# Matrix balancing on 32 partitions against 128 partitions in two halves, at the head of a fused attention and gated-MLP kernel

## The chip, the core and the metric

The kernel runs on one core of a Trainium2 chip. A core has a matrix engine (TensorE, "PE" in the profile, with its weight loads as "PEld"), a vector engine (VectorE, DVE), an activation engine (ScalarE, ACT), a general engine (GpSimd, POOL) and a synchronisation engine (SyncE, SP), each with an instruction queue of its own that it works through in order, and 16 DMA engines that all queues share. Matrix products land in PSUM, which PE alone writes by products and which ACT and DVE read; everything else lives in SBUF. The metric is the device time of one execution in microseconds (us). The kernel before takes 232.88 us, the median of three runs (232.8 to 232.88).

## What is computed

The reference balances a small 8x8 matrix for each of 4 batches x 8 heads by five rounds of exponential, row normalisation and column normalisation. The result mixes the eight blocks (96 positions each) of the keys and of the values; block-diagonal attention follows, and then a two-layer gated MLP.

```python
P = sort_net                                   # (4, 8, 8, 8)
for _ in range(5):
    P = P - np.max(P, axis=-1, keepdims=True)
    P = np.exp(P)
    P = P / (np.sum(P, axis=-1, keepdims=True) + 1e-09)
    P = P / (np.sum(P, axis=-2, keepdims=True) + 1e-09)
...
k_sorted = np.einsum('bhij,bhjcd->bhicd', P, k_b)
v_sorted = np.einsum('bhij,bhjcd->bhicd', P, v_b)
scores = scale * np.matmul(q_b, k_sb.transpose(0, 1, 2, 4, 3))
attn = exp(scores - rowmax) / (rowsum + 1e-09)
x = attn @ v_sb                                # 3072 tokens x 512
h = x @ w_in                                   # 512 x 2048
out = (h * np.cos(h)) @ w_out                  # 2048 x 512
```

## The kernel before

The 3072 tokens go in eight chunks `n` of 384, two for each batch; a chunk has four blocks `u` of 96 positions. The order of the instructions on every engine is the order in which the program text issues them. The text from line 77 to line 990 or so is the head of the kernel: inputs are loaded, the matrices are balanced, the keys and values of batch 0 are mixed, and attention of chunk 0 is computed. With `up_four(0, 0, 0)` (line 982) begins the MLP of chunk 0, and from there on pieces of attention for later chunks are placed between the MLP's products.

**Balancing.** `P` (line 80) holds one (batch, head) pair on each of 32 partitions, 64 numbers in a row. `rounds(it)` (line 334) runs five times: an exponential on ACT, then `normalize` (line 307), six DVE instructions: sum, reciprocal, product for the rows, and the same for the columns. The last product writes `sorted_by` in bf16. To bring the 8x8 matrices of 16 (batch, head) pairs into the block-diagonal form that a product over 128 partitions needs, `block` (line 380) makes eight products of 8 columns with the 0/1 matrices `pick`, built on POOL (`picked`, line 211), and `spread` (line 391) multiplies the result with the mask `maskp` into `bds[0]` (keys), `bdv` (values) and, much later (line 1024), `bds[1]` (batches 2 and 3). Between these steps the rounds carry other work: `q_twice` and `q_place` (transposes of q for chunk 0 on PE, copies on ACT), the clearing of halves of `kbuf` and `vbuf` on POOL, loads of `w_in`, and `idle(...)`, products without use on PE.

**Loads.** All large loads are issued on POOL's queue and converted to bf16 on the way: `load_q(0)`, K and V of batch 0 (lines 190 to 192), then three quarters of `w_in`, held back by a copy (`held`, line 368) that waits for a column reciprocal of the second round, the fourth quarter behind the fourth round, `load_q(1)` (line 378), four pieces of `v_permute`, `w_out` (lines 925 to 930), and K and V of batch 1 (lines 968 and 970). `P` itself comes on SP's queue.

**Keys, values, scores.** `kp` (line 744) multiplies 16 columns of keys with `bds[0]` into a PSUM tile; `k_place` copies it to `kT` on ACT or DVE, in two parts `half` for the first and last four blocks. `s_ps`, `s_max` and `s_sub` make the scores of a block, their row maxima, and the differences; `expo` makes the exponential. `expo(..., True)` leaves the transposing of the probabilities to PE (`p_ps`) and a copy (`p_ev`); without `True` it issues a DMA transpose on SP's queue. `v0` and `v0e` mix the values of batch 0; `av_products`, `av_norm` (line 614 on), `x_ps` and `x_ev` make the attention output and its transpose for the MLP. `q_products(1, 0, ...)` at line 977 transposes the second load of q on PE.

**PSUM.** Two pools: `big` with three tiles of two banks, `acc` with two tiles of one bank. A tile is given out again when its last reader in program order has passed.

Of the kernel before, what the change touches and what calls it, by code (L numbers as in the profile page):

```python
# [18 lines left out]
def kernel(  # L19
# [15 lines left out]
    nc = tc.nc  # L35
# [155 lines left out]
    load(kbuf, 64, kin_d[0])  # L191
    load(vbuf, 0, vin_d[0])
    make_identity(nc, ident[:])
# [5 lines left out]
    zero_words(nc.gpsimd, kbuf[:64, :CD // 3])  # L199
# [4 lines left out]

    def pick_at(z, n):
        return pair[:B * H, z * PB * nb:(z + n) * PB * nb].rearrange(
            "p (j c) -> p j c", j=nb)

    pick, pick_pair = pick_at(0, 2), pick_at(2, 2)

    def picked(t, z, b):

        nc.gpsimd.affine_select(
            out=t[:, :, z * PB:(z + 1) * PB], in_=t[:, :, z * PB:(z + 1) * PB],
            compare_op=ALU.not_equal, fill=1.0, base=-b * PB,
            pattern=[[1, nb], [-1, PB]], channel_multiplier=nb)

    def picks(t, batches):
        nc.gpsimd.memset(t[:], 0.0)
        for z, b in enumerate(batches):  # L220
            picked(t, z, b)
# [10 lines left out]
    nc.vector.memset(pick[:], 0.0)  # L232
# [7 lines left out]

    early = const.tile([128, 1], FP32, name="early")
    nc.scalar.activation(early[:], half_pi[:], AF.Exp)

# [6 lines left out]
    keep_warm(14, big.tile([128, 512], FP32, name="idle", tag="big"))  # L250
# [32 lines left out]
    E_eps = const.tile([B * H, nb, nb + 1], FP32, name="E")  # L283
    Q_eps = const.tile([B * H, nb + 1, nb], FP32, name="Q")
    E, Q = E_eps[:, :, :nb], Q_eps[:, :nb]
    top = const.tile([B * H, nb], FP32, name="top")
    less = const.tile([B * H, nb, nb], FP32, name="less")
    sums = [const.tile([B * H, nb], FP32, name=f"sums{z}") for z in range(2)]
    over = [const.tile([B * H, nb], FP32, name=f"over{z}") for z in range(4)]
    sorted_by = const.tile([B * H, nb, nb], BF16, name="sorted_by")  # L290
    maskp = const.tile([128, 2 * H], FP32, name="maskp")
    bds = [const.tile([128, 2 * H, nb], BF16, name=f"bd{g}") for g in range(NG)]
    bdv = const.tile([128, 2 * H, nb], BF16, name="bdv")
    held = const.tile([128, 1], FP32, name="held")

    def by_row(t):
        return t.to_broadcast([B * H, nb, nb])

    def by_column(t):
        return t[:].unsqueeze(1).to_broadcast([B * H, nb, nb])  # L300

    nc.vector.memset(E_eps[:, :, nb:], 1e-9)
    nc.vector.memset(Q_eps[:, nb:], 1e-9)
    nc.vector.reduce_max(top[:], P[:], axis=AX.X)
    nc.vector.tensor_tensor(less[:], P[:], by_row(top), op=ALU.subtract)

    def normalize(it, out):

        nc.vector.reduce_sum(sums[0][:], E_eps[:], axis=AX.X)
        nc.vector.reciprocal(over[0][:], sums[0][:])  # L310
        nc.vector.tensor_tensor(Q, E, by_row(over[0]), op=ALU.mult)
        nc.vector.reduce_sum(sums[1][:], Q_eps.rearrange("p i j -> p j i"), axis=AX.X)
        nc.vector.reciprocal(over[(1, 2, 1, 3, 1)[it]][:], sums[1][:])
        nc.vector.tensor_tensor(out, Q, by_column(over[(1, 2, 1, 3, 1)[it]]), op=ALU.mult)

    turns = {}

    def q_twice(h2):
        ps = turns[h2] = acc.tile([128, 2, IC, QR, blk // QR], BF16, name="qps", tag="acc")
        for hp in range(2):  # L320
            for r in range(QR):
                for x in range(2):
                    nc.tensor.transpose(
                        ps[x * D:(x + 1) * D, hp, :, r],
                        q_rows[:, h2 * 2 + hp, r * D:(r + 1) * D], ident[:blk, :blk])

    def q_place(h2):
        dst = q_turned[0][:, :, :QW].rearrange("d e (i h c) -> d h e i c", h=H2, c=blk)
        A.copy(dst[:, h2], turns.pop(h2).rearrange("d e i r p -> d e i (r p)"))
# [4 lines left out]
    def rounds(it):  # L334
        nc.scalar.activation(E, less[:], AF.Exp)
        if it == 0:
            A.copy(
                order.rearrange("k (p r) -> k p r", r=QR),
                ident[:blk, :blk].rearrange("k (r p) -> k p r", r=QR))
            q_twice(0)  # L340
            q_twice(1)
            idle(4)
        if it == 3:
            q_place(0)
            q_twice(2)
            idle(2)
            q_place(1)
            q_twice(3)
            idle(2)
        if it == 4:  # L350
            q_place(2)
            q_place(3)
        if it in (1, 2):
            n = (D - 12 - VN) // 2 * blk
            t = vperm[64:, VN * blk + (it - 1) * n:VN * blk + it * n].bitcast(FP32)
            A.copy(t, nones[64:].to_broadcast([64, n // 2]))
# [894 lines left out]
```

## Time and profile before

| what | before |
|---|---|
| median of three runs | 232.88 us |
| span of the profiled execution, first to last instruction | 231.6 us |
| PE busy | 223.5 us (97%) |
| DVE busy | 170.9 us (74%) |
| ACT busy | 154.2 us (67%) |
| POOL busy | 95.9 us (41%) |
| bytes moved by DMA | 31.21 MB |

The span is that of one profiled execution; its time outside the span isn't given by itself, so the difference to the median, 1.3 us, stands for what lies around it. A row of the timeline has the start and the duration in us, the engine, the line of the program, the operation, output and inputs, shapes and a count; in brackets stands how long the engine was idle before and what released it. Idle time of an engine that isn't the bound costs nothing.

### The profile page before, as it was taken

How to read it: one execution, taken by the hardware profiler on the slowest of the kernel's cores; microseconds unless marked ns; L12 is line 12 of the kernel's file. 1: busy time of each engine (PE TensorE's matmuls, PEld its weight loads, DVE VectorE, ACT ScalarE, POOL GpSimd, SP SyncE). 2: the span in 40 equal slices, each digit the busy share in tenths (PEclk: the TensorE clock that was granted, in tenths of full speed). 3: DMA queues.
4: the chain of work that ended last, by engine and by line, in shares of the span. 5: the costliest groups of instructions: out<-in, count | busy, mean ns of one | idle time of the engine just before them, and what ended most of it. 6: DMA issues, size and time to landing. Idle time of an engine off the chain costs nothing.

```text
span 231.6 us, 5534 instructions
## 1 busy us (share of the span) xinstructions
PE 223.5 (97%) x2268; PEld 138.9 (60%) x2268; DVE 170.9 (74%) x291; ACT 154.2 (67%) x207; POOL 95.9 (41%) x121
## 2 busy tenths in 40 slices
PE   8888999999999999999999999999999999999994
PEld 3477898567665566644666456555655566556553
DVE  6769968978789778877389986997699769745700
ACT  5658877777789858794888566746675666716521
POOL 7999999399950188932709000900000000000000
PEclk9999999999999999999999999999999999999999
DMA  5999999994999999797989839964923450351012
GB/s 69 230 191 207 202 207 233 199 225 139 125 135 172 174 137 148 130 168 158 154 138 89 122 72 146 215 90 92 207 91 69 90 167 0 68 146 45 0 45 93
DMA packets 67673, 31.21 MB, mean 135 GB/s; under 512 B 56384, under 2 KB 63168, under 8 KB 67392
## 3 DMA queue, kind: packets, MB, share of 16 engines
q0 software_dynamic: 24048, 13.64, 43.5%
q1 hardware_dynamic: 43312, 17.02, 35.1%
q8 instruction: 18, 0.29, 0.5%
q10 hardware_dynamic: 288, 0.20, 0.3%
q14 instruction: 7, 0.06, 0.1%
HBM read 27.27 MB, written 6.29 MB: 145 GB/s over the span
## 4 chain that ended last, share of the span: by engine, by line
PE 85%; DMA 5%; DVE 3%; POOL 2%; ACT 2%; issue 1%; SPq 1%; POOLq 0%; ACTq 0%
PE h L669 30%; PE o L694 28%; PE h L857 5%; PE o L878 5%; DMA kTs<-kTs 4%; PE av L625 3%; PE sc L438 3%; PE ks L408 2%; PE o L1215 2%; PE pps L835 1%; PE xps L656 1%; PE sc L504 1%; PE vs L782 1%; PE xps L844 1%; SPq L421 1%
## 5 line engine op out<-in xcount | busy, mean ns | idle before, releaser
L669 PE MATMUL h<-xT,w_in_t 128*128 128x384 bf16 x448 | 78.4, 326 | 0.0
L694 PE MATMUL o<-w_out_t,gg 128*128 128x512 bf16 x320 | 76.2, 379 | 0.0
L677 DVE TENSOR_TENSOR gg<-c,h 128x768 bf16<-128x768 f32 x56 | 52.7, 949 | 20.0 <-ACT c L673 20.0
L673 ACT ACTIVATE c<-h,half_pi 128x768 f32<-128x768 f32 x56 | 50.4, 900 | 25.3 <-PE h L669 24.4
L669 PEld LDWEIGHTS <-w_in_t 128*128 128x128 bf16 x448 | 42.2, 98 | 26.5 <-DMA xT<-xn 0.4
L694 PEld LDWEIGHTS <-gg 128*128 128x128 bf16 x320 | 28.9, 98 | 28.4
L179 POOL COPY vperm<-kv 64x768 bf16<-64x768 bf16 (+2 forms) x12 | 28.4, 2413 | 3.9 <-DMA kv<-in_v_dram 3.9
L570 ACT ACTIVATE p_buf<-s 96x768 bf16<-96x768 f32 x32 | 26.6, 842 | 5.1 <-DVE s L491 4.0
L489 DVE TENSOR_REDUCE mx<-sc 96x4 f32<-96x384 f32 (+1 forms) x33 | 24.0, 728 | 2.2 <-PE sc L504 2.2
L491 DVE TENSOR_TENSOR s<-sc,mx 96x384 f32<-96x384 f32 (+1 forms) x33 | 24.3, 735 | 1.6
L638 DVE TENSOR_TENSOR xn<-av,r 96x512 bf16<-96x512 f32 x32 | 22.0, 686 | 1.1
L129 POOL DMA_DIRECT2D kv<-in_q_dram x24 | 16.0, 680 | 0.8 <-issue 0.5
L257 ACT COPY kv<-o 128x512 f32<-128x512 f32 (+2 forms) x10 | 5.2, 523 | 14.1 <-PE o L694 11.5
L257 ACT CAST kTs<-ks 128x512 bf16<-128x512 f32 (+1 forms) x18 | 11.0, 630 | 5.3 <-PE ks L408 4.4
L636 DVE RECIPROCAL r<-av 96x8 f32<-96x8 f32 x32 | 6.4, 199 | 7.9 <-PE av L625 7.6
L878 PE MATMUL o<-w_out_t,gg 128*128 128x512 bf16 x48 | 11.7, 379 | 0.0
L438 PE MATMUL sc<-kTs,q_turned 128*128 128x96 bf16 x152 | 11.0, 206 | 0.5 <-DMA kTs<-kTs 0.5
L129 POOL DMA_DIRECT2D q_mem<-in_q_dram x16 | 10.7, 690 | 1.8 <-DMA kv<-in_v_dram 1.5
L259 DVE COPY kv<-o 128x512 f32<-128x512 f32 (+1 forms) x5 | 3.1, 612 | 11.1 <-PE o L1215 8.5
L857 PE MATMUL h<-xT,w_in_t 128*128 128x192 bf16 x128 | 11.1, 246 | 0.0
L438 PEld LDWEIGHTS <-q_turned 128*128 128x128 bf16 x152 | 8.8, 98 | 3.0 <-issue 0.6
L857 PEld LDWEIGHTS <-w_in_t 128*128 128x128 bf16 x128 | 10.5, 98 | 0.0
(134 smaller groups left out, 279.1 us busy)
## 6 DMA issues: line engine op xcount, KB each, us to landing
out_dram<-kv SPq DMA_DIRECT2D x12, 256.0 KB, 2.6
out_dram<-o_s SPq DMA_DIRECT2D x10, 256.0 KB, 3.1
w_in_t<-in_moe_w_in_dram POOLq DMA_DIRECT2D x4, 512.0 KB, 11.8
w_out_t<-in_moe_w_out_dram POOLq DMA_DIRECT2D x4, 512.0 KB, 12.4
kv<-in_k_dram POOLq DMA_DIRECT2D x2, 768.0 KB, 9.9
kv<-in_v_dram POOLq DMA_DIRECT2D x2, 768.0 KB, 13.0
pair<-in_k_dram POOLq DMA_DIRECT2D x2, 768.0 KB, 12.4
kv<-in_v_dram POOLq DMA_DIRECT2D x6, 256.0 KB, 5.7
```

Source lines behind the costliest of these rows:

```text
L129: nc.gpsimd.dma_start(out=q_heads[:, i, :, e], in_=src[:, ih * IC + i, :, e])
L179: nc.gpsimd.tensor_copy(dst, src)
L438: nc.tensor.matmul(out, q_of(n, hp)[:, x:x + 128], keys_of(n, u, h2, hp), start=True, stop=True)
L489: nc.vector.reduce_max(mx[:], scv, axis=AX.X)
L491: nc.vector.tensor_tensor(s, scv, mx.to_broadcast(list(s.shape)), op=ALU.subtract)
L570: nc.scalar.activation(p[:, :, :blk], s_t.pop((n, u)).rearrange("p e h c -> p (e h) c"), AF.Exp, scale=scale)
L669: nc.tensor.matmul(h[:, f2, :w], w_in_t[:, kk, f * 128:(f + 1) * 128], xT[n][:, kk], start=(kk == 0), stop=(kk == KC - 1))
L673: nc.scalar.activation(c[:], h[:, :, :w], AF.Sin, bias=half_pi[:, 0:1])
L677: nc.vector.tensor_tensor(gt[n, fp // 2][:, f:f + 2], c[:], h[:, :, :w], op=ALU.mult)
L694: nc.tensor.matmul(o[:], gt[n, f // 4][:, f % 4, ts * 128:(ts + 1) * 128], w_out_t[:, f, :], start=(f == 0), stop=(f == FC - 1))
L857: nc.tensor.matmul(o[:, part, f2 * w:(f2 + 1) * w], w_in_t[:, kk, f * 128:(f + 1) * 128], xT[0][:, kk, h * w:(h + 1) * w], start=(kk == 0) ...
L878: nc.tensor.matmul(out_ps[ts][:], gt[0, q][:, f % 4, ts * 128:(ts + 1) * 128], w_out_t[:, f, :], start=(f == 0), stop=(f == FC - 1))
```

## The change

`P` is loaded with one (batch of a pair, head, row) on each of 128 partitions, and the two pairs of batches (`g` = 0, 1) beside each other with 8 numbers each. The first exponential takes the row maximum as bias. The row sums of the first round are then sums along a partition; a product with a 128x128 fp32 matrix (`wide`) turns the matrices, so that from there on rows are columns: the column sums are sums along a partition, and their reciprocal becomes the scale of the next exponential, while the row sums are fp32 products with a 0/1 block matrix (`own`). The small constant of the reference enters through a product with ones (`start_rows`) ahead of each. The two halves take turns. The last reciprocal is multiplied in with the mask, so that `bds[0]` and `bds[1]` come directly out of the last round; `block`, `pick`, `bdv` and the later `picks` go. One matrix `bds[0]` serves keys and values.

Keys of batch 0 now lie on the first 64 partitions of `kbuf` and those of batch 1 on the others. Key copies use four PSUM tiles (16, 16, 8 and 8 columns) instead of three of 16. The probabilities of blocks 0 and 3 of chunk 0 are transposed by DMA instead of PE. The first warm-up has 9 products instead of 14, and the later `idle` and `fill` products of the head go. Some clearings move from POOL to DVE (`ident`, `p_bufs`, the ones in `vS`) or from ACT to DVE (half of a stretch of `vperm`), and ahead of the K and V loads POOL gets four small additions (`tree`).

```diff
-    P = const.tile([B * H, nb, nb], FP32, name="P")
-    nc.sync.dma_start(out=P.rearrange("p i j -> p (i j)"),
-                      in_=sort_net.rearrange("b h i j -> (b h) (i j)"))
+    P = const.tile([128, NG, nb], FP32, name="P")
+    nc.sync.dma_start(
+        out=P[:], in_=sort_net.rearrange("(g b) h i j -> (b h i) g j", g=NG))
...
     load_q(0)
-    load(kbuf, 64, kin_d[0])
+    nc.vector.memset(ident[:], 0.0)
+    nc.gpsimd.affine_select(
+        out=ident[:], in_=ident[:], compare_op=ALU.not_equal, fill=1.0, base=0,
+        pattern=[[-1, 128]], channel_multiplier=1)
+    tree = [const.tile([128, w + w // 8], FP32, name=f"tree{w}") for w in (64, 32, 16, 8)]
+    nc.vector.memset(tree[3][:, nb:], 0.0)
+    t = ident
+    for x, w in zip(tree, (64, 32, 16, 8)):
+        nc.gpsimd.tensor_tensor(x[:, :w], t[:, :w], t[:, w:2 * w], op=ALU.add)
+        t = x
+    place9 = tree[3]
+    load(kbuf, 0, kin_d[0])
     load(vbuf, 0, vin_d[0])
-    make_identity(nc, ident[:])
...
-    nc.vector.memset(pick[:], 0.0)
...
+    for t in p_bufs:
+        nc.vector.memset(t[:, :, blk:], 0.0)
...
-    keep_warm(14, big.tile([128, 512], FP32, name="idle", tag="big"))
+    keep_warm(9, big.tile([128, 512], FP32, name="idle", tag="big"))
...
+    def start_rows(g, lo, n):
+        nc.tensor.matmul(
+            turned[g][:, lo:lo + n], every, least[:, lo:lo + n], start=True, stop=False)
...
+    def turn_first(g):
+        nc.vector.reduce_sum(sums[:, g, 0:1], first[:, g], axis=AX.X)
+        nc.vector.reciprocal(over[:, g, 0:1], sums[:, g, 0:1])
+        shape = [128, 2 * H, nb]
+        nc.vector.scalar_tensor_tensor(
+            wide[g].rearrange("p (c j) -> p c j", j=nb),
+            first[:, g, :nb].unsqueeze(1).to_broadcast(shape), over[:, g, 0:1],
+            maskn.to_broadcast(shape), op0=ALU.mult, op1=ALU.mult)
+        start_rows(g, 0, nb + 1)
+        nc.tensor.matmul(
+            turned[g][:, :nb + 1], wide[g], place9[:], start=False, stop=True)
+
+    def columns(g, it, x):
+        nc.vector.reduce_sum(sums[:, g, it:it + 1], x, axis=AX.X)
+        nc.vector.reciprocal(over[:, g, it:it + 1], sums[:, g, it:it + 1])
+
+    def exp_next(g, it):
+        x = turned[g] if it == 1 else Q[g]
+        nc.scalar.activation(
+            E[g][it % 2][:], x[:, :nb], AF.Exp, scale=over[:, g, it:it + 1])
+
+    def add_rows(g, it):
+        start_rows(g, RS + (it - 1) * nb, nb)
+        nc.tensor.matmul(
+            turned[g][:, RS + (it - 1) * nb:RS + it * nb], own, E[g][it % 2][:],
+            start=False, stop=True)
+
+    def rows(g, it):
+        nc.vector.reciprocal(
+            rows_over[:, g], turned[g][:, RS + (it - 1) * nb:RS + it * nb])
+        nc.vector.tensor_tensor(
+            Q[g][:, :nb], E[g][it % 2][:], rows_over[:, g], op=ALU.mult)
...
+    for it in range(2, 5):
+        for g in range(NG):
+            rows(g, it - 1)
+            columns(g, it, Q[g][:])
+            exp_next(g, it)
+            add_rows(g, it)
+            if it == 2 and g == 1:
+                q_twice(0, 0, *C)
+                q_twice(0, 1, *C)
+            if it == 3:
+                q_twice(1, g, *C)
+                q_place(0, g, A)
+            if it == 4:
+                z, x = ((2, B), (3, C))[g]
+                q_twice(z, 0, *x)
+                q_twice(z, 1, *x)
+                q_place(1, g, A)
         if it == 4:
-            q_place(2)
-            q_place(3)
...
+            nc.gpsimd.tensor_copy(held[:], over[:, 0, 3:4])
+            for z in range(3):
                 load_w_in(z)
...
+    last_round(0)
+    spread(0, 0, H)
+    q_place(2, 0, A)
+    q_place(2, 1, A)
+    nc.gpsimd.memset(
+        vbuf[64:].bitcast(FP32).rearrange("p (c d) -> p c d", d=D // 2)[:, :, :VN // 2],
+        0.0)
+    load_w_in(3)
     load_q(1)
...
-    kp(2, *B)
-    kp(0, *B)
+    kp(32, 16, *B)
+    kp(0, 16, *B)
+    kp(16, 8, *C)
+    kp(24, 8, *C)
...
-    k_place(2, A, 1)
-    k_place(2, V, 0)
-    kp(1, *B)
+    q_place(3, 0, V)
+    q_place(3, 1, V)
+    k_place(32, V, 0)
     k_place(0, A, 0)
-    blocks.append(block([pick[:, :, z * PB:(z + 1) * PB] for z in (1, 0)]))
-    k_place(1, V, 0)
-    k_place(1, A, 1)
-    values_matrix()
+    k_place(16, V, 0)
+    k_place(24, A, 0)
+    k_place(16, V, 1)
+    k_place(24, A, 1)
+    last_round(1)
+    s_ps(0, 0)
+    v_ones()
+    spread(0, H, 2 * H)
+    spread(1, 0, 2 * H)
+    v0(0, *C)
+    v0(4, *C)
     k_place(0, A, 1)
-    s_ps(0, 0, fill=3)
-    v0(4, *C)
+    k_place(32, A, 1)
     s_max(0, 0)
-    v0(0, *B)
...
-    ones(0)
-    expo(0, 0, True)
+    expo(0, 0)
...
-    expo(0, 3, True)
-    v0(3, *B, fill=2)
+    expo(0, 3)
+    v0(3, *B)
...
-    p_ps(0, 0, *C, fill=2)
...
-    p_ev(0, 0, V)
...
-    p_ps(0, 3, *C)
...
-    p_ev(0, 3, A)
...
-    load(kbuf, 0, kin_d[1])
+    load(kbuf, 64, kin_d[1])
...
-    picks(pick_pair, (2, 3))
...
-    p_pads()
...
-    last = block([pick_pair[:]], *C)
...
-    spread(bds[1], last)
```

More of the change, by code (lines that the diff above doesn't have):

```diff
@@ L203 @@
     PB = H * nb
[L205 to L221, printed above, removed]
     vS[0] = const.tile([blk, 4 * NB, VW], BF16, name="vS")
@@ L281, in q_place_half @@
                 q_ps[n, z][rows].rearrange("d e i r p -> d e i (r p)"))
[L283 to L289, printed above, removed]
@@ L302 @@
[L302 to L314, printed above, removed]
@@ L316 @@
-    turns = {}
[L318 to L327, printed above, removed]
+    room = pair.bitcast(FP32)
+    wide = [room[:, g * 128:(g + 1) * 128] for g in range(NG)]
@@ new lines @@
+    every, own = room[:, 256:384], room[:, 384:512]
+    least = const.tile([128, RS + 4 * nb], FP32, name="least")
+    first = const.tile([128, NG, nb + 1], FP32, name="first")
+    E = [[const.tile([128, nb], FP32, name=f"E{g}{z}") for z in range(2)] for g in range(NG)]
+    Q = [const.tile([128, nb + 1], FP32, name=f"Q{g}") for g in range(NG)]
+    top = const.tile([128, NG], FP32, name="top")
+    sums = const.tile([128, NG, 6], FP32, name="sums")
+    over = const.tile([128, NG, 6], FP32, name="over")
@@ L948 @@
     kxp(2)
-    v0(2, *B, fill=1)
-    p_ev(0, 0, V)
+    v0(2, *B)
     v0e(7, A)
```

158 lines of the change are left out of this document (73 added, 85 removed).

## The prediction

> **What bounds the kernel now.** I read the busy times of long stretches first, to see where TensorE leaves room.
>
> ```profile
> span 231.6 us, 5534 instructions
> 0.00:28.00 28.00, 24.10 (x390) 16.61 (x391) 21.58 (x68) 19.04 (x35) 25.76 (x39) 1.00 1.06 179
> 28.00:50.00 22.00, 22.00 (x272) 17.51 (x270) 17.34 (x24) 17.15 (x22) 18.07 (x21) 1.00 1.15 213
> 50.00:100.00 50.00, 49.52 (x576) 31.27 (x574) 40.92 (x68) 39.20 (x54) 35.06 (x36) 1.00 1.00 151
> ```
>
> The columns are stretch, length, then busy time of PE, weight loads, DVE, ACT and POOL, the clock, the DMA share and GB/s. From 28 us on PE is full. So a delay ahead of the first up-projection reaches the end whole, and after it only PE work counts. The change lies ahead of it, so I read the first 28 us engine by engine.
>
> ```profile
> 1.71 0.54 DVE L197 MEMSET vperm<- 64x576 f32 x1 [0.16 <-issue]
> 2.47 0.21 DVE L304 TENSOR_REDUCE top<-P 32x8 f32<-32x64 f32 x1
> 4.81 0.26 ACT L335 ACTIVATE E<-less 32x64 f32<-32x64 f32 x1 [0.56 <-DVE pair L359]
> 5.10 0.22 DVE L309 TENSOR_REDUCE sums<-E 32x8 f32<-32x72 f32 x1 [0.18 <-ACT E L335]
> 5.57 0.21 DVE L311 TENSOR_TENSOR Q<-E,over 32x64 f32<-32x64 f32 x1
> 6.94 0.22 DVE L309 TENSOR_REDUCE sums<-E 32x8 f32<-32x72 f32 x1 [0.37 <-ACT E L335]
> 12.24 0.36 PE L386 MATMUL bl<-sorted_by,pair 32*128 32x8 bf16 x8 [0.69 <-POOL held L368]
> 12.64 0.22 DVE L393 TENSOR_TENSOR bd<-maskp,bl 128x64 bf16<-128x64 f32 x1 [0.54 <-PE bl L386]
> 12.91 1.56 PE L408 MATMUL ks<-bd,kv 128*128 128x64 bf16 x48 [0.31 <-DVE bd L393]
> 16.12 0.95 DVE L821 TENSOR_REDUCE mx<-sc 96x8 f32<-96x768 f32 x1 [0.25 <-PE sc L801]
> 23.02 0.94 DVE L825 TENSOR_TENSOR s<-sc,mx 96x768 f32<-96x768 f32 x1
> 27.19 0.56 PE L268 MATMUL qps<-ident,q_mem 96*64 96x96 bf16 x16
> 27.68 0.34 PE L844 MATMUL xps<-order,xn 96*128 96x96 bf16 x4
> 27.86 3.47 PE L857 MATMUL h<-xT,w_in_t 128*128 128x192 bf16 x40
> ```
>
> A round lasts 6.94 - 5.10 = 1.84 us, nearly all DVE. From the first reduction (2.47) to the block matrix (12.86) are 10.4 us; the first score maximum follows 3.3 us later, the last subtraction (L825) ends at 23.96, the first up-projection starts at 27.86. The `q_products` just ahead of it need the second load of q:
>
> ```profile
> 12.91 0.81 POOL L119 DMA_DIRECT2D q_mem<-in_q_dram  x1
> q_mem<-in_q_dram POOLq DMA_DIRECT2D x1, 384.0 KB, 14.2
> 14.00:27.10 13.10, 1.00 1.27 206
> ```
>
> That load landed at 12.91 + 14.2 = 27.1 us, under 0.1 us before its use, out of a queue that moved some 206 GB/s all the time (last row: DMA share and GB/s). So there are two chains to the dense stage, engines and loads, and both arrive together. Making one shorter gains nothing; making either longer costs.
>
> **Start of the rounds.** DVE takes over the clearing of the identity, of the three `p_bufs` pads and of a second stretch of `vperm`, and gets a 128x128 tile of ones; it loses a 0.48 us clearing of `pick`. At the 0.54 us per 576 words of L197 the `vperm` part is 0.45 us, the pads, 128 words each, about 0.15 us each, the ones 0.15 us, the rest 0.2 us: 0.8 us more net, so the first reduction starts at 3.3 us instead of 2.47. `P` now comes in 256 runs of 32 bytes:
>
> ```profile
> P<-in_sort_net_dram SPq DMA_DIRECT2D x1, 8.0 KB, 1.7
> ```
>
> Issued at 0.75, it landed by 2.47. At twice that latency it would come at 4.2. Bounds for the start: +0.3 (clearings overlap) to +1.7; I take +0.8.
>
> **The rounds.** The DVE rows here cost 0.21 to 0.22 us for 64 or 72 elements, with 0.03 us between; for 8 or 9 elements I take 0.17, so 0.81 us for the four operations of a half (reciprocal, product, sum, reciprocal; between 0.7 and 1.0). Two halves are 1.62 us. The loop of one half is 0.81 + 0.1 to ACT + 0.23 (the exponential of 64 elements is 0.26) + one fp32 product with its hand-overs. No fp32 product stands in the trace. Nearest is L386: eight weight loads and eight products of 8 columns in 0.36 us. Bounds are one such alone, 0.17 us, and 0.8 us, twice the group; I take 0.5 us. The Trainium skill (FP8 and Floating Point Precision, TensorE Precision Notes) counts four passes for a true fp32 product; half of the eight passes of L386 would give about 0.2 to 0.3 us as an estimate, and the sum would fall by some 0.6 us.
>
> So an alternation is about 1.7 us, no shorter than a round by more than 0.14. There are three; the first turn is longer (exponential, sum, reciprocal, a 128-wide product, fp32 product, sum, reciprocal, exponential, product: 3.6 us from the first reduction). The last round and the spreading are 1.1 us. PE also has to do the q transposes between the fp32 products:
>
> ```profile
> 6.83 0.87 PE L323 MATMUL qps<-ident,q_mem 96*64 96x96 bf16 x32
> ```
>
> Sixteen are 0.44 us, and the other half's product queues behind them: 0.5 us. Sum 3.6 + 3 x 1.72 + 0.5 + 1.1 = 10.4 us, what it is now. The removed `block` products with their hand-overs (0.54 us) are in that comparison. Bounds 9.7 (no queueing, products at the low bound) to 13 (six products on the path at 0.8, and queueing behind the other half's). Key products then start 0.8 us later.
>
> **Keys to first maximum.** Separate tiles let ACT and DVE copy the middle third at once, instead of ACT waiting 0.87 us for DVE:
>
> ```profile
> 14.19 1.29 DVE L259 CAST kTs<-ks 128x512 bf16<-128x512 f32 x2 [1.33 <-ACT kTs L257]
> 15.51 1.07 ACT L257 CAST kTs<-ks 128x512 bf16<-128x512 f32 x2 [0.87 <-DVE kTs L259]
> 28.32 0.34 DVE L259 COPY xT<-xps 128x384 bf16<-128x384 bf16 x1
> ```
>
> But DVE now has, between the first spreading and the first maximum, two q copies (0.34 us each, as the `xT` copy), key copies of 0.64 (half of the row of two) + 2 x 0.38 (half as many columns), the other half's last round 0.81, a column of ones and two spreadings 0.7, with 0.3 of waiting for the products: 3.9 us against 3.3. That is +0.6.
>
> **First maximum to dense stage.** Two of four probabilities go through a DMA transpose, so one copy leaves DVE (0.54) and one ACT (0.84):
>
> ```profile
> 22.56 0.54 DVE L259 COPY pT<-pps 96x768 bf16<-96x768 bf16 x1
> 24.74 1.68 ACT L257 COPY pT<-pps 96x768 bf16<-96x768 bf16 x2
> L257 ACT CAST vS<-vs 96x512 bf16<-96x512 f32 x8 | 4.6, 592 | 0.9 <-PE vs L782 0.7
> L570 ACT ACTIVATE p_buf<-s 96x768 bf16<-96x768 f32 x4 | 3.4, 844 | 0.0
> ```
>
> ACT has eight value copies and four exponentials there, 4.6 + 3.4 = 8.0 us, and is about as full as DVE with its eight operations of 0.95; so I count -0.5 for the DVE copy and nothing for ACT's. Chain of engines: +0.8 + 0 + 0.6 - 0.5 = +0.9, dense stage at 28.8.
>
> **The loads.** On POOL the K load now stands behind the identity's selection and four adds; with 0.25 us each K is issued 1.3 us later, and its first bytes are missing while the queue starts:
>
> ```profile
> 3.58 0.29 POOL masks.py:199 TENSOR_SCALAR_AFFINE_SELECT ident<-ident 128x128 bf16<-128x128 bf16 x1
> 8.27 2.32 POOL L160 DMA_DIRECT2D w_in_t<-in_moe_w_in_dram  x3
> 4.00:5.00 1.00, 1.00 1.26 158
> ```
>
> With only q in flight at 4 to 5 us, I take 0.5 us of the stream as lost (bounds 0 and 1.3). The w_in loads wait for the third sums instead of the second round and are issued at about 9.5 instead of 8.3; V is then still under way, so the queue doesn't run dry. The two transposes come on top, through the same 16 DMA engines:
>
> ```profile
> 60.00:75.00 15.00, 1.00 1.08 136
> q1 hardware_dynamic: 3366, 0.85, 31.0%
> q_turned<-kv SPq DMA_TRANSPOSE x2, 7.3
> pT<-p_buf SPq DMA_TRANSPOSE x2, 3.9
> ```
>
> Four transposes took 31% of 15 us, 1.16 us each of all engines; two are 2.3 us ahead of the second q. As packet times overlap there (shares above 1), I count half, 1.1 us (bounds 0 and 2.3). Second q: 27.1 + 0.5 + 1.1 = 28.7; plus the 0.67 us of L268 and L844 ahead of L857, and 0.1, the dense stage starts at 29.5 (27.9 to 31.5). It is the later of the two chains: +1.6. The transposes themselves (3.9 us under load) have about 5 us until `av_products`: no term, 1 to 3 us if they take the 7.3 of the row above them.
>
> **Dense stage.** It loses the products of batches 2 and 3:
>
> ```profile
> 37.86 0.37 PE L386 MATMUL bl<-sorted_by,pair 32*128 32x8 bf16 x8
> ```
>
> In a full PE that is -0.3. The POOL work that goes (`picks`, `p_pads`) hid behind PE and is worth nothing. If later loads shift by 1.6 us too, the second K comes at about 42.5, before its use at 43.5.
>
> **Sum.** +1.6 - 0.3 = +1.3 us. The profiled span is 231.6 us, the runs' median 232.88, so 1.3 us lie around it and stay: **234.2 us**.
>
> **Rivals.** *Faster, by arriving sooner.* If the transposes overlap the stream wholly and the fp32 products are cheap, both chains arrive as now or up to 0.4 us sooner, and with the 0.3 us of L386 the time is 232.88 - 0.3 - 0.2 = 232.4 at the edge and 231.9 at best. For it: DVE's waits (0.2 to 0.4 us a round) can be filled by the other half. Against: the second q can't land sooner from a full queue that starts later.
>
> *Same.* Chain and loads are late by only 0.1 to 0.7 us and the 0.3 us gives it back: 232.6 to 233.3.
>
> *Slower by the clock.* PE's warm-up shrinks from 14 products to 9, and eight more in the rounds and the later fills go:
>
> ```profile
> 1.00 5.90 PE L246 MATMUL idle<-warm 128*128 128x512 bf16 x14 [1.00 <-DVE warm L231]
> 7.64 1.04 PE L246 MATMUL idle<-warm 128*128 128x512 bf16 x4
> ```
>
> Now 14 take 0.42 us each and the next four 0.26: PE sped up after about 5.5 us of dense work. Nine end at about 5 us, perhaps before that. Were PE slow until the key products, these 48 would take 3.1 us instead of 1.56, the scores and fp32 products double too (about 1.5): 234.2 + 3 = 237. It decides if the granted clock is not full by 10 us. The Trainium skill (TensorE: Matmul & The Clock Gate, Part 1) has the full clock granted after a busy window of 3.4 us whose phase is free; nine products, 3.8 us, fill such a window only by luck.
>
> **How the numbers follow.** Loads or chain late (233.4 to 235.8): 0.50. Clock or a late transpose: 0.15. Same: 0.13. Faster: 0.22. Slower is 0.65 in all; 0.2% is about what this kernel's measurement can tell from no change. The likeliest case's own range is 233.3 to 235.8; to hold 8 in 10 it goes down into the faster case and up towards the slow clock: 232.0 to 236.5.
>
> **What would show it.** First reduction near 3.3 us; alternations of 1.7 us; key products near 13.7; PE waiting for the DMA of q at `q_products`, up-projection near 29.5. Wrong, if q lands by 27.5 or an alternation is under 1.5 us; the clock, if PE's first transposes run at half speed.

## The result, and the profile after

The changed kernel takes 266.43 us (median of four runs, 263.41 to 270.0) beside 232.88 us (four runs, 232.8 to 233.24): a ratio of 1.1331, interval 1.1265 to 1.1396. Two of the four runs (267.51 and 270.0) are in a slower state, and the ratio goes by the other two, 263.41 and 265.35. It is slower, as forecast, but by some 31 us instead of 1.3. The page of the changed kernel, its span, the share of PE in 40 slices of 6.6 us, and the granted clock in tenths:

```profile
span 263.6 us, 5505 instructions
...
PE   8997530059999989999999999999999999999995
...
PEclk9555555557999999999999999999999999999999
```

PE is nearly empty in slices 6 to 8 and runs at half clock in slices 2 to 9, two things that the page of before had nowhere. Stretches of the changed kernel, columns as in the prediction (clock, DMA share and GB/s last):

```profile
0.00:28.00 28.00, 23.78 (x274) 19.95 (x275) 19.67 (x77) 13.82 (x33) 21.85 (x34) 0.63 1.06 173
28.00:58.40 30.40, 6.94 (x94) 6.17 (x93) 6.61 (x13) 5.43 (x11) 10.38 (x13) 0.50 0.91 123
...
62.00:100.00 38.00, 37.01 (x485) 27.49 (x483) 29.94 (x44) 27.71 (x39) 23.96 (x23) 1.00 0.65 108
```

From 62 us on PE is full again at full clock, as before from 28. The loss lies ahead of that. The landmarks, in the timeline of the changed kernel:

```profile
3.31 0.17 DVE L312 TENSOR_REDUCE top<-P 128x2 f32<-128x16 f32 x1
16.24 2.74 PE L435 MATMUL ks<-bd,kv 128*128 128x64 bf16 x48
23.36 0.94 DVE L842 TENSOR_REDUCE mx<-sc 96x8 f32<-96x768 f32 x1
29.96 0.95 DVE L846 TENSOR_TENSOR s<-sc,mx 96x768 f32<-96x768 f32 x1
36.73 1.12 PE L652 MATMUL av<-vS,pT 96*128 96x65 bf16 x16 [5.91 <-DMA pT<-p_buf]
56.00 0.65 PE L652 MATMUL av<-vS,pT 96*128 96x65 bf16 x8 [17.10 <-DMA pT<-p_buf]
58.46 5.19 PE L878 MATMUL h<-xT,w_in_t 128*128 128x192 bf16 x40
```

Against the rows of before, the key products start 3.33 us later (16.24 - 12.91), the first maximum another 3.91 later (7.12 us behind them instead of 3.21), the differences then take 0.29 less (end at 30.91, before 23.96). Then PE waits 5.91 and 17.10 us for the two DMA transposes, 23.0 us; the other 0.65 us of that stretch is a remainder, products at half clock among it. The first up-projection is 30.6 us late, and its first 40 products take 5.19 us instead of 3.47. What follows them is 0.3 us shorter (199.95 us to the end of the span, before 200.27). That is 3.33 + 3.91 - 0.29 + 23.0 + 0.65 + 1.72 - 0.3 = 32.0 us, all of the difference of the spans (263.6 - 231.6).

So there were three things to explain: the landing of the transposes, the clock, and the 3.91 us ahead of the first maximum.

### The profile page after: what moved, and what is told of

It is laid out like the page before. It is cut to its first block, busy times and chain, and to the rows that moved or that the text cites. A ratio compares the mean times of both kernels' runs of the same rounds, so it can differ in the third digit from the quotient of the medians.

```text
span 263.6 us, 5505 instructions
## 1 busy us (share of the span) xinstructions
PE 231.6 (88%) x2237; PEld 150.0 (57%) x2237; DVE 175.3 (66%) x311; ACT 154.6 (59%) x214; POOL 91.7 (35%) x114
## 4 chain that ended last, share of the span: by engine, by line
PE 77%; DMA 14%; DVE 6%; ACT 1%; issue 1%; SPq 0%; DVEq 0%; ACTq 0%
PE h L696 27%; PE o L721 24%; DMA pT<-p_buf 11%; PE h L878 5%; PE o L899 4%; PE av L652 3%; PE sc L465 2%; PE ks L435 2%; DMA vperm<-p_buf 2%; DMA kTs<-kTs 1%; PE o L1234 1%; PE qps L359 1%; PE turned L341 1%; PE turned L309 1%; DVE mx L842 1%
## 5 line engine op out<-in xcount | busy, mean ns | idle before, releaser
L721 PE MATMUL o<-w_out_t,gg 128*128 128x512 bf16 x320 | 76.2, 379 | 0.0
L704 DVE TENSOR_TENSOR gg<-c,h 128x768 bf16<-128x768 f32 x56 | 52.7, 949 | 20.4 <-ACT c L700 20.4
L696 PEld LDWEIGHTS <-w_in_t 128*128 128x128 bf16 x448 | 42.3, 98 | 26.3 <-DVE xT L257 0.3
L652 PE MATMUL av<-vS,pT 96*128 96x65 bf16 x120 | 7.1, 209 | 23.0 <-DMA pT<-p_buf 23.0
L652 PEld LDWEIGHTS <-pT 96*128 96x128 bf16 (+1 forms) x144 | 7.4, 109 | 25.6 <-DMA pT<-p_buf 23.4
L119 POOL DMA_DIRECT2D q_mem<-in_q_dram x3 | 2.5, 841 | 35.0 <-PE qps L266 31.8
L255 ACT COPY xT<-xps 128x384 bf16<-128x384 bf16 x5 | 2.4, 479 | 20.7 <-PE xps L865 18.3
L255 ACT CAST kTs<-ks 128x512 bf16<-128x512 f32 (+2 forms) x19 | 11.1, 607 | 5.8 <-PE ks L435 5.7
L878 PE MATMUL h<-xT,w_in_t 128*128 128x192 bf16 x128 | 12.8, 267 | 0.0
L878 PEld LDWEIGHTS <-w_in_t 128*128 128x128 bf16 x128 | 12.0, 107 | 0.3
## 6 DMA issues: line engine op xcount, KB each, us to landing
w_out_t<-in_moe_w_out_dram POOLq DMA_DIRECT2D x4, 512.0 KB, 12.6
```

The source lines that it names most:

```text
L255: eng.copy(dst, src)
L652: nc.tensor.matmul(a[:w, hp, h2 * (D + 1):(h2 + 1) * (D + 1)], pt[:blk, e * blk:e * blk + w], vS[g][:, v_at(g, b2, hp, h2, ih * IC + u), : ...
L696: nc.tensor.matmul(h[:, f2, :w], w_in_t[:, kk, f * 128:(f + 1) * 128], xT[n][:, kk], start=(kk == 0), stop=(kk == KC - 1))
L704: nc.vector.tensor_tensor(gt[n, fp // 2][:, f:f + 2], c[:], h[:, :, :w], op=ALU.mult)
L721: nc.tensor.matmul(o[:], gt[n, f // 4][:, f % 4, ts * 128:(ts + 1) * 128], w_out_t[:, f, :], start=(f == 0), stop=(f == FC - 1))
L878: nc.tensor.matmul(o[:, part, f2 * w:(f2 + 1) * w], w_in_t[:, kk, f * 128:(f + 1) * 128], xT[0][:, kk, h * w:(h + 1) * w], start=(kk == 0) ...
```

## The experiments

**Transposes back on PE (e1), fillers back (e2), both (e3), transposes alone put into the kernel before (e4).** The theory on top was that the transposes are starved; its rival, that PE at half clock delays all and the waits only show it.

```diff
 e1: -    expo(0, 0)              -    expo(0, 3)
     +    expo(0, 0, True)        +    expo(0, 3, True)
     +    p_ps(0, 0, *C), p_ev(0, 0, V), p_ps(0, 3, *C), p_ev(0, 3, A) where the kernel before has them
 e2: -    keep_warm(9, ...)
     +    keep_warm(14, ...)
     +            idle(2)      # in each half's turn of rounds 2 to 4, behind its row product
     +    s_ps(0, 0, fill=3), v0(3, *B, fill=2), v0(2, *B, fill=1), av_products(0, 3, fill=2)
 e4 (kernel before):
     -    expo(0, 0, True)        -    expo(0, 3, True)
     +    expo(0, 0)              +    expo(0, 3)
     -    p_ps(0, 0, ...), p_ev(0, 0, V), p_ps(0, 3, *C), p_ev(0, 3, A)
     -    p_pads()                # their pads are cleared on DVE instead, behind the first spreading
```

> The changed kernel with the two DMA transposes of probabilities (blocks 0 and 3 of chunk 0) given back to TensorE and their copies to DVE and ACT. Theory 'transposes' (the two DMA transposes share the 16 DMA engines with large loads, land 10 and 28 us after issue, and TensorE waits 23 us for them, whatever the clock is): the 23 us go, the clock stays at half until the dense stage; up-projection near 36 us, time 240 to 245 us. Theory 'clock' (the waits are only where the slow matrix engine shows; the clock is the cause): time above 255 us, the waits turn up elsewhere.

> The changed kernel with products without use put back: 14 instead of 9 at the start, 2 behind each fp32 row-sum product of the three alternations, and those of the score and value stage. The DMA transposes stay. Theory 'transposes': the clock is full before 28 us, the chain to the probabilities is 3 to 6 us shorter, but the waits for the two transposes stay at 18 us or more; time 252 to 262 us. Theory 'clock': time 233 to 237 us.

> Both edits of the two kernels before this together: probabilities turned on TensorE and the products without use put back. Theory 'transposes and clock, each a cost of its own': the changed balancing alone is left; up-projection at 28 to 30 us, time 232.5 to 235.5 us. If a third cost is hidden (loads, key copies), above 236 us.

> The kernel before with one part of the change alone: the probabilities of blocks 0 and 3 of chunk 0 are transposed by DMA, the pads of the probability buffers cleared on DVE ahead of that. The clock is full there and the warm-up as before. Theory 'transposes': the second transpose lands more than 15 us after its issue, and the time is above 245 us. Theory 'clock': the transposes land in 3 to 8 us, time 232 to 236 us.

Measured, with the kernel before at 233.7 us beside them: e1 245.01 us, e2 266.56, e3 245.14 (ratio 1.0493, 1.0459 to 1.0526), e4 241.46 (e1, e2 and e4 one run each). Taking the two transposes off the DMA queue shortens the span by 20.4 us (263.6 to 243.2). The fillers alone give nothing: the waits stay, only 4 us shorter, and the fillers themselves make the rounds longer. PE's waits in e2, its clock from 9.6 to 26.8 us, and its key products, 6 us later than in the changed kernel:

```profile
PE av L653 <- DMA pT<-p_buf: 18.9, 2, 13.3
...
9.60:26.80 17.20, 16.66 (x162) 12.63 (x164) 7.50 (x30) 6.17 (x16) 9.52 (x10) 0.52 1.13 184
...
22.22 2.77 PE L436 MATMUL ks<-bd,kv 128*128 128x64 bf16 x48
```

So e2 did not bring the clock back, against its expectation, and says nothing on what a full clock would give. That the clock alone is not the cause is shown by e1, where the waits go though the rounds stay slow, and by e4, where the clock is full until PE waits for the transposes. The transposes alone cost the kernel before 7.8 us, less than the starvation theory expected and more than its rival. The packets of the two queues in e4, from 25 to 27 us (queue: packets, MB, share of 16 engines), the time from issue to landing, and PE's waits:

```profile
q0 software_dynamic: 476, 0.25, 89.7%
q1 hardware_dynamic: 474, 0.12, 45.6%
...
DMA to landing us min/median/max: 9.0/10.7/12.4
...
PE av L627 <- DMA pT<-p_buf: 6.9, 2, 4.4
```

A transpose is some 800 small packets (two are 1600, 0.39 MB), and here they go out one for one with the packets of the load beside them: 474 and 476. The same count in the changed kernel, from 33 to 37 us, beside the `w_out` loads, and from 40 to 50 us, beside K and V of batch 1, which POOL issues at 31.86 and 32.39; then the landings:

```profile
q0 software_dynamic: 633, 0.63, 92.7%
q1 hardware_dynamic: 635, 0.15, 30.0%
...
DMA packets 413, 1.14 MB, mean 114 GB/s; under 512 B 288, under 2 KB 329, under 8 KB 329
q0 software_dynamic: 149, 1.07, 72.3%
q1 hardware_dynamic: 264, 0.06, 18.6%
...
kv<-in_v_dram POOLq DMA_DIRECT2D x1, 768.0 KB, 27.9
pT<-p_buf SPq DMA_TRANSPOSE x1, 27.9
```

Beside `w_out`, whose packets are 1 KB (0.63 MB / 633), the transposes get 159 packets a microsecond. Beside K and V they get 26. Of the 413 packets there, 84 are of 8 KB or more, and these carry nearly all of the 1.07 MB, some 12 KB each. The turns are not one for one there (264 beside 149), so the packet counts show which stream slows the transposes, but not by what rule. In e4 the second transpose landed at 33.4 us, with load packets of 1 KB beside it to the end (585, 0.58 MB, in the last 3.4 us); in the changed kernel, issued 7 us later, it ran into K and V. That could explain most of the difference between 241 and 266, and e6 tests it.

**Only K and V of batch 1 held back until the second transpose has landed (e6).** What POOL issues behind them moves too.

```diff
+    p_hold(0, 3)      # a POOL copy that reads the transposed block
     load(kbuf, 64, kin_d[1])
```

> The changed kernel with one edit: POOL waits for the second DMA transpose (a copy of one element of its output) ahead of the loads of K and V of batch 1. Theory 'the second transpose starves beside the K and V loads with their large packets': it lands 4 to 7 us after the first instead of 19, the up-projection starts 12 to 15 us sooner, time 250 to 255 us; the first transpose stays at 9 to 11 us, beside the w_out loads. Rival 'the transposes are slow by themselves here': the second lands 15 us or more after the first, time 264 us or more.

It takes 249.43 us (one run). Issue to landing of its two transposes, and its first up-projection:

```profile
DMA to landing us min/median/max: 10.0/11.3/12.6
...
43.15 4.23 PE L878 MATMUL h<-xT,w_in_t 128*128 128x192 bf16 x40
```

The second lands after 12.6 us instead of 27.9, PE's wait for it falls from 17.10 to 2.25 us, and the span is 16.0 us shorter (247.6): the loads of K and V beside it are shown to be the cause of that part. That it is the size of their packets is what the counts above suggest; no run changed the size alone. The first still takes 10.0 us beside `w_out`, and PE still waits 5.44 us for it.

**The clock.** With the transposes on PE, e1 and e3 are still 11 us behind. Two rows of e1 on PE, then two stretches of e3:

```profile
1.08 4.02 PE L244 MATMUL idle<-warm 128*128 128x512 bf16 x9 [1.08 <-DVE half_pi L224]
...
37.16 5.28 PE L878 MATMUL h<-xT,w_in_t 128*128 128x192 bf16 x40
```

```profile
6.40:9.60 3.20, 2.62 (x20) 2.31 (x18) 1.67 (x10) 0.62 (x3) 1.32 (x2) 1.00 0.94 188
9.60:26.80 17.20, 16.40 (x149) 12.44 (x149) 7.42 (x32) 6.27 (x17) 9.26 (x10) 0.50 1.13 188
```

In e1 nine warm-ups end without a faster clock (4.02 us for nine, 0.45 each), and all rounds go at half speed. The clock column cannot show that: it reads 1.00 for e1 from 4 to 20.3 us and for e7 below from 5 to 16.8, ahead of the first change of clock in their traces, so there the half is read from the rows, 48 key products in 2.74 and 2.72 us instead of 1.56. In e3 fourteen bring it, but from 6.4 to 9.6 us PE has fp32 products of 8 columns alone, the clock falls, and then it stays at a half for 17.2 us though PE counts as busy for 16.4 of them. e3 missed its 232.5 to 235.5 by 10 us: it brought the fillers back, but behind the stretch in which the clock is lost. So e5 puts one product of 512 columns ahead of each row product, in place of the one that adds the constant (from here on the kernels built on it, e5 and e8 to e11, leave the constant out of these sums), and e7 does the opposite in the kernel before.

```diff
 e5 (on e1, with the later fills of e2):
     -        start_rows(g, 0, nb + 1)      -        start_rows(g, RS + (it - 1) * nb, nb)
     +        idle(1)                       +        if (it, g) != (4, 1): idle(1)
 e7 (kernel before):
     -    keep_warm(14, ...)      -            idle(4)      -                idle(2)
     +    keep_warm(9, ...)
```

> The changed kernel with probabilities turned on TensorE, the products without use of the score and value stage put back, and each fp32 product of the small constant (start_rows; the kernel leaves the constant out of the row sums) replaced by one bf16 product of 512 columns without use. Warm-up stays at 9. Theory 'fp32 products of 8 columns fill TensorE's time but don't hold its clock': full clock from the first 7 us to the end, alternations of 1.4 to 1.7 us, up-projection at 27.5 to 29.5 us, time 232 to 235.5 us. Rival 'the clock is lost by the shorter warm-up alone': clock at half from about 5 to over 20 us as without it, time above 240 us.

> The kernel before with 9 products of warm-up instead of 14 and without the eight further products without use in the rounds; nothing else is changed, no fp32 products. Theory 'fewer long products lose the clock, whatever the balancing': half clock for some 10 us or more before the dense stage, time 235 to 240 us. Rival 'the fp32 products lose it, the shorter warm-up costs nothing': clock full from about 7 us on, time 232.8 to 234 us.

e5 takes 237.52 us beside 233.46 (two runs, ratio 1.0175, 1.0029 to 1.032, too wide to say by how much it is slower; 232 to 235.5 was expected), e7 236.57 (one run). The timeline of e5: the first half's reciprocal at both ends of the three alternations, the key products, and what follows on DVE, with the POOL copies beside it:

```profile
6.94 0.21 DVE L347 RECIPROCAL rows_over<-turned 128x8 f32<-128x8 f32 x1
...
12.05 0.21 DVE L347 RECIPROCAL rows_over<-turned 128x8 f32<-128x8 f32 x1
...
13.71 1.56 PE L436 MATMUL ks<-bd,kv 128*128 128x64 bf16 x48 [0.46 <-DVE bd L373]
...
15.28 5.86 POOL L179 COPY vperm<-kv 64x768 bf16<-64x768 bf16 x4
16.05 0.73 DVE L349 TENSOR_TENSOR Q<-E,rows_over 128x8 f32<-128x8 f32 x1
17.42 0.87 DVE L373 SCALAR_TENSOR_TENSOR bd<-Q,over,maskp 128x64 bf16<-128x64 f32 x1 [0.24 <-issue]
18.21 1.59 DVE L373 SCALAR_TENSOR_TENSOR bd<-Q,over,maskp 128x128 bf16<-128x128 f32 x1
19.73 0.94 DVE L843 TENSOR_REDUCE mx<-sc 96x8 f32<-96x768 f32 x1
```

With the clock kept through the rounds (from 20 to 28.5 us it is 0.80 in mean), the three alternations take 5.11 us, 1.70 each, and the key products start at 13.71. Against e1, the up-projection starts 5.4 us sooner (31.72), and its first 40 products take 3.46 us instead of 5.28: 7.3 of the 8.8 us between the spans (243.2 and 234.4). Which share of this is the clock, which the products dropped with the constant, and which the later fills isn't told apart; the dropped products are 0.22 to 0.25 us each at full clock. In e7 PE goes at half speed until some 17 us and the up-projection starts at 29.39 instead of 27.86: of its 3.1 us lost, 1.5 are that later start; the rest wasn't followed.

**The first maximum.** It comes 6.02 us behind the key products in e5 (3.21 in the kernel before). Three DVE rows above do not fit: L349 takes 0.73 us where the same operation took 0.17 in every round, L373 takes 0.87 and, for twice the columns, 1.59 where its first call took 0.28. All three read two SBUF operands while POOL copies. The kernel before has spreadings beside the same copies, but with one operand in PSUM; its rows:

```profile
14.02 5.88 POOL L179 COPY vperm<-kv 64x768 bf16<-64x768 bf16 x4 [0.30 <-DMA kv<-in_v_dram]
15.40 0.21 DVE L393 TENSOR_TENSOR bdv<-maskp,bl 128x64 bf16<-128x64 f32 x1
```

e8 moves the other half's product, sum and two spreadings into the dense stage, where POOL doesn't copy.

```diff
 (on e5; two fillers instead of three at the first scores, two more at the first p_ps)
-    last_round(1)           -    spread(0, H, 2 * H)      -    spread(1, 0, 2 * H)
+    rows_over of half 1 right behind spread(0, 0, H)
     gate_four(1, 2)
+    rest()                  # product, sum, reciprocal, and the two spreadings
```

> The kernel with the small constant's products replaced (TensorE turns, full clock) and one edit more: of the second half's last round only the reciprocal stays ahead of the scores (right behind the first block matrix); its product, sum, reciprocal and the two spreadings, which took 0.73, 0.16, 0.16, 0.87 and 1.59 us there, move into the dense stage, where they are needed first by the key products of batch 1. Theory 'these small DVE operations were slow because POOL's copies into vperm ran beside them, and they stood ahead of the first score maximum': in the new place, where POOL runs no copies, they take 0.17, 0.16, 0.16, 0.3 and 0.4 us; the first maximum comes 3 us sooner, at 16.2 to 17 us, the up-projection at 28 to 29.5 us, time 232.5 to 234.5 us. Rival 'they are slow by their shape and operands': the same durations in the new place. Rival 'the second load of q sets the dense stage': it lands at 27.4 to 28 us, and the up-projection can't start before 28.2.

It takes 235.68 us (ratio 1.009, 1.0059 to 1.0121; 232.5 to 234.5 was expected). The moved instructions in its timeline (the last row is both spreadings), then its clock from 10 to 20 us and its key products:

```profile
39.42 0.16 DVE L924 TENSOR_TENSOR Q<-E,rows_over 128x8 f32<-128x8 f32 x1
...
39.89 0.53 DVE L373 SCALAR_TENSOR_TENSOR bd<-Q,over,maskp 128x64 bf16<-128x64 f32 x2
...
10.00:20.00 10.00, 9.64 (x132) 8.25 (x134) 5.54 (x23) 5.57 (x14) 8.71 (x9) 0.53 1.11 196
...
15.22 2.74 PE L437 MATMUL ks<-bd,kv 128*128 128x64 bf16 x48
```

0.16 and 0.53 us, for what took 0.73 and 2.46 in e5: it is the place, not the shape. That it is POOL's reading there, and no other neighbour, rests on the rows of the kernel before and wasn't tried by moving the copies.

The first maximum did not come at 16.2 to 17 us, as expected, but at 19.37. In this execution the clock fell at some 9 us, although its rounds have the same products as those of e5. So one product of 512 columns beside each small one does not hold the clock every time, and the difference between e5 and e8 is not the price of the move.

**What is left (e9, e10, e11).** e9 takes several clearings ahead of the first reduction off DVE and has two fillers instead of one in the first alternations. e10 and e11 also issue K and V ahead of the identity. e10 puts the second q ahead of the last `w_in` load; e11 puts it behind again, with the release of the `w_in` loads one column sum sooner.

```diff
 e9  (on e8):  p_bufs' pads to POOL, later; a stretch of vperm to ACT; two fillers in the first alternations, one instead of two at the turn
 e10 (on e9):  load_q(0); load K; load V; then the identity       load_q(1) ahead of load_w_in(3)
 e11 (on e9):  as e10 for K and V; load_w_in(3) ahead of load_q(1)
-            nc.gpsimd.tensor_copy(held[:], over[:, 0, 3:4])
+            nc.gpsimd.tensor_copy(held[:], over[:, 0, 2:3])
```

> The kernel with the late rest of the second half, and four edits more that the runs point to: the pads of the probability buffers cleared on POOL in the dense stage, the second stretch of vperm cleared on ACT, the ones and the small constants of the removed products not written (so that DVE's first reduction needs only P), and two instead of one product without use ahead of the row sums of the first two alternations. The small constant is left out of the row sums as before. Theory 'start of DVE and the clock's windows were what was left': first reduction at 2.5 instead of 3.3 us, no half-clock stretch after 10 us, up-projection at 27.5 to 28.5 us, time 231.8 to 233.2 us, equal to the kernel before or up to 1 us faster. Rival 'TensorE's warm-up sets the first turn anyway': first turned product not before 4.9 us, time 233 to 235 us, as the kernel before or slower.

> The kernel before this one with two changes of order on POOL: the loads of K and V of batch 0 stand ahead of the identity and its four additions again (as in the kernel before the change), and the second load of q stands ahead of the last quarter of w_in. Theory 'V came 1.3 us late, and so POOL's pieces of vperm and the value products of TensorE, which waited 0.6 to 0.7 us three times and lost its clock in that stage': V lands at 14 instead of 15.2 us, no such waits, full clock from 20 to 26 us, up-projection at 27 to 28.3 us (from 30.3), time 232 to 233.3 us, equal to the kernel before on this chip or up to 0.8 us faster. Rival 'the identity comes too late for the first turn': first turned product after 5.5 us, time 234 us or more.

> The kernel with K and V loaded ahead of the identity, the second load of q behind the last quarter of w_in again, and one edit more: the first w_in loads wait for the second column sums instead of the third. Theory 'POOL's queue itself was late: behind the wait for the third sums (to 9.3 us) came three loads, a clearing, two more loads, and only at 15.0 us the first piece of vperm': the wait ends at about 7.9 us, the first piece starts at 13.9 to 14.4 us, the value products don't wait for it, the clock stays full from 18 to 25 us, up-projection at 27.5 to 28.5 us, time 232.3 to 233.6 us. Rival 'the clock is lost in that stage anyway, since TensorE has too little to do between the first scores and the probabilities': half clock for 3 us or more between 15 and 28 us, time above 234 us.

Times and ratios: e9 234.83 us, 1.0055 (1.0036 to 1.0075), e10 235.9, 1.0103 (1.0066 to 1.014), e11 233.69, 1.0026 (1.0007 to 1.0044). e9 and e10 missed their expectations. In both the clock held through the rounds and fell in the value stage (a mean of 0.88 over the first 28.5 us). In e9 the value products waited 0.59 to 0.73 us, three times, for POOL's copies of V. In e10 V came sooner, but POOL reached the copies at 15.03 us because the release of the loads still held it to 9.28. In e11 the release comes at 7.86 and the copies begin at 14.32; the value products still wait for them, 0.46 and 0.69 us, which its theory had excluded, but the clock stays full from the rounds on (1.00 over the first 28.5 us):

```profile
13.00 1.56 PE L434 MATMUL ks<-bd,kv 128*128 128x64 bf16 x48
...
15.48 0.95 DVE L841 TENSOR_REDUCE mx<-sc 96x8 f32<-96x768 f32 x1 [0.36 <-PE sc L821]
...
27.17 0.56 PE L262 MATMUL qps<-ident,q_mem 96*64 96x96 bf16 x16 [0.19 <-DMA q_mem<-in_q_dram]
...
27.84 3.47 PE L877 MATMUL h<-xT,w_in_t 128*128 128x192 bf16 x40
```

The first maximum is 0.64 us sooner than in the kernel before (15.48 against 16.12), and the up-projection starts where it did (27.84 against 27.86). Of the 0.64 us, 0.28 are left at the last `av` products (26.57 against 26.85), and then PE waits 0.19 us for the second q. No version ran faster than the kernel before, those without the constant included.

## Why the prediction was right and wrong

**The step that failed** is the last one on the loads: "The transposes themselves (3.9 us under load) have about 5 us until `av_products`: no term". The five us were there (the first was issued at 26.20, PE had nothing else from 30.82 on), but the two took 10.5 and 27.9 us, and the term is 23.0 us of waiting. The mechanism was named (a late transpose, at 1 to 3 us), its size was not seen. The 3.9 us had not been measured under load: those transposes were issued from 73.41 us on in the kernel before, and from there to 77.3 us the trace has 1143 packets of the transposes' queue and none of a load. The 7.3 us are little better, with 90 load packets beside 3130 while their packets went out (69.2 to 73.4 us). Ahead of `av_products` the transposes had load packets beside them, first of 1 KB and then of 12. The bytes were counted (2.3 us of all engines), when what set the time was 1600 packets that had to wait among those of a load. The Trainium skill (DMA: Bandwidth & Descriptors, Queues, rings and completion order) states that an engine takes turns between its queues packet by packet; 635 beside 633 agrees, 264 beside 149, with K and V, does not by count.

So the sign of the forecast came out right for another reason than the one given: the 1.6 us of late loads that it rests on were not what held PE up.

**The clock** was given 3 us and, with a late transpose, 0.15. The condition came true (half clock at 10 us), and it was worse than put: it wasn't late but lost again at some 7 us, and it stayed down until 62. By the landmarks it accounts for at most 2.5 us in the rounds (12.9 us from the first reduction to the key products, 10.4 in e5, which also drops the constant's products), 1.18 us of the key products (2.74 against 1.56) and 1.72 us of the first up-projections. The argument looked only at when nine warm-ups end; it left out that the first rounds behind them hold nothing but products of 8 columns. For the kernel before, its 3 us came out, but in part by luck: e7 loses 3.1, of which only 1.5 lie ahead of the dense stage.

**Keys to first maximum** was put at 3.9 us and took 7.1, and still 6.0 in e5 at full clock. "A column of ones and two spreadings 0.7" was one error: the two spreadings alone are 2.46 us, and the product ahead of them 0.87 instead of 0.17. The rows of the changed kernel, first in a round, then beside POOL's copies:

```profile
6.84 0.17 DVE L348 TENSOR_TENSOR Q<-E,rows_over 128x8 f32<-128x8 f32 x1
...
17.45 5.83 POOL L179 COPY vperm<-kv 64x768 bf16<-64x768 bf16 x4
19.57 0.87 DVE L348 TENSOR_TENSOR Q<-E,rows_over 128x8 f32<-128x8 f32 x1
```

The nearest spreading that the prediction shows, L393 at 0.22 us, has one operand in PSUM. The Trainium skill (SBUF — State Buffer, Who interferes with whom) says that a DVE instruction with two SBUF inputs contends with a GpSimd instruction that reads SBUF, and not with one that only writes it. This trace agrees on both: 0.87 us beside the copies, 0.17 at 6.84 beside a clearing (POOL's memset from 4.99 to 7.72).

**What held.** The start at 3.3 us (3.31, no wait for `P`). The alternation of 1.7 us and key products at 13.7, at full clock: 1.70 and 13.71 in e5, with a filler in place of the constant's product, so the halves gain nothing over the old rounds, as argued. The fp32 product with its hand-overs was taken at 0.5 us: in e5 0.47 us lie between the end of the first exponential behind the turn (6.47) and the reciprocal that reads its product (6.94). In the changed kernel, with two products there, they are 0.78 (5.82 to 6.60), which the sum did not count. A product alone costs 0.22 to 0.25 us, by the distance of the changed kernel's rows at full clock:

```profile
6.44 0.39 PE L309 MATMUL turned<-least,pair 128*128 128x8 f32 x2
6.69 0.37 PE L341 MATMUL turned<-E,pair 128*128 128x8 f32 x2
6.91 0.37 PE L309 MATMUL turned<-least,pair 128*128 128x8 f32 x2
```

That agrees with the prediction's estimate for a product alone, 0.2 to 0.3 us. From the first maximum to the last difference it is 0.3 us less (0.5 was put).

**The loads** as the later chain, second q at 28.7: q landed at 28.7 in the changed kernel, by luck, and nobody waited for it there. It was issued at 16.62 us instead of 12.91, 2.32 us of it because POOL waited for PE's slow q transposes, and took 12.1 us instead of 14.2; the DMA transposes, counted at 1.1 us ahead of it, sent no packet before 30 us. The row behind these 1.1 us was read for four transposes alike, but 3130 of its 3366 packets belong to two transposes of q. e11 shows the gate where nothing else is late, with 0.19 us of waiting at `q_products`. No run bore out the rival that the change arrives sooner: in e11 the engines were ahead, and q landed at 27.2 us, as before.

## What to carry to other kernels

A DMA that is made of many small packets takes turns with the queues that run beside it, so a small transpose beside a load is priced by the load's packets, not by its own bytes; and a latency that is carried over has to come from a stretch with the same load beside it. Before work is taken from a busy engine, look at what its neighbours read while the moved instruction runs: its row has to come from the same operands beside the same neighbour. And fillers that look like waste are priced by what the clock does without them, in the first stretch that holds small products alone, and over several executions, as the clock can hold in one and fall in the next.

## What the runs showed of the hardware that was not expected

Beside a running load, a transpose's first packet goes out 3.8 to 4.8 us after its issue, with nothing ahead of it on SP's queue: issued at 26.20 in the changed kernel, no packet of `q1` up to 30 us and 58 from 30 to 31; issued at 19.22 in e4, none up to 23. With no load beside it, issued at 73.41 in the kernel before behind two others, all but one of its first 51 packets go out from 74.4 to 74.7. A transpose also slows what it runs beside: K and V of batch 1, queued behind `w_out` in both, landed 24.9 and 27.9 us after issue in the changed kernel and 11.7 and 14.8 in the kernel before, which has no transposes there.

Being busy doesn't bring the clock. In the changed kernel PE counts as busy for all of the 5 us from 10 to 15, at half clock:

```profile
10.00:15.00 5.00, 5.00 (x49) 4.57 (x47) 2.51 (x14) 2.87 (x9) 4.26 (x5) 0.50 0.97 185
```

The Trainium skill (TensorE: Matmul & The Clock Gate, Part 1) lets the clock follow how busy PE was in a window of free phase. The phase agrees: the same nine warm-ups took 3.54 us in the changed kernel, with full clock from 4 us, and 4.02 in e1, without. But being busy by the profile is not enough for the gate. One 512-column product beside each small one kept the clock through the rounds in e5's profiled execution and lost it at some 9 us in e8's; two in the first alternations kept it in those of e9, e10 and e11, one execution each. Where the bound lies, and what of this is the phase, wasn't tried.
